# A fixed order for the first phase of a packed-attention and mixer kernel

## The chip, the cores and the metric

The kernel runs on one core of one Trainium2 chip. The metric is the device time of one execution in microseconds. A core has TensorE (matrix products and transposes, called PE in the profile), VectorE (DVE), ScalarE (ACT), GpSimd (POOL) and SyncE (SP), which only issues transfers; each runs its own instructions in its own order, and they wait for each other by semaphores. Transfers run on 16 DMA engines.

## The reference

Inputs: `q`, `k`, `v` of 8 batches x 8 heads x 576 rows x 64, and `p` of 32 rows for each head; matrices `U` (576 x 32), `V` (32 x 576), `w_ch1` (512 x 2048) and `w_ch2` (2048 x 512), these four in float64. For every batch:

```python
p_packed = sm_attn(p, k, v)            # softmax(scale * p k^T) v, 32 rows per head
out = sm_attn(q, p_packed, p_packed)   # 576 rows per head
x = out.transpose(0, 2, 1, 3).reshape(B, S, H * D)
u = x + (x^T U V)^T                    # mixing over the 576 tokens
y = u + relu(u @ w_ch1) @ w_ch2        # the output, float32
```

## The kernel before

**The first phase** computes `p_packed`. Its unit is half a batch: four heads, so there are 16 units (`UN`), two for each batch. A unit goes through these stages:

- `a_load`, `a_load_v`: K is loaded in one transfer (line 190, tile `kx`), V in five (lines 391 and 392, tile `vt`); with the first unit of a batch also the rows of `p`, in two (line 381, `pn`). K and V have three buffers each.
- `a_turn`: K is transposed on TensorE in three groups (lines 201 and 208, into `k_ps`) and copied out to `kT` by ScalarE (lines 205 and 209); with the first unit of a batch also `p` (`a_p`).
- `a_scores` (line 219): 16 small products into `s_ps`. `a_softmax` (lines 421 to 425): maxima on VectorE, exponentials on ScalarE.
- `a_turn_back` (lines 226 and 228): the exponentials are transposed back into `m_ps` and copied to `eT`.
- `a_pack` (line 451): 40 small products with V; ScalarE scales them to `two` (line 453).
- `a_heads` (line 461): one transpose, copied out by ScalarE (line 462). After the second unit of a batch other than the first, the packed rows are stored in DRAM (line 467, `ppTd`), from where `load_ppT` fetches them later.

Beside the units the phase loads `w_ch1` in 16 chunks of 512 KB (`load_w1`, line 136, issued from ScalarE) and makes float32 of them (`convert_w1`, through `float32_of`: the Abs of line 76 on ScalarE, then lines 77 to 80 on VectorE). Four chunks are in flight: two tiles `bits` and two `bits2`. It prepares `U` and `V`, does the second attention and the token mixing of batch 0 (`attention(0)`, 24 steps, called `first`), and the first piece of the folded weight (`fold(0, 0)`: the packed rows times `w_ch1`). In this phase the program's text gives no order: a planner with a cost model reorders each engine's instructions, SyncE's too, within what the data and the free buffers allow.

**The second phase** is in the order of the source (`tc.manual_schedule()`), on every engine. It loops over 8 batches and, in each, over 16 blocks `kt` of the hidden dimension. `gemm1(kt)` makes 128 hidden values of all rows from the batch's attention weights and the folded weight, split into high and low parts, so each product is three (lines 85 to 87); `gemm2(kt - 1)` multiplies by `w_ch2`. Among these products stand the steps of the next batch's attention (`steps`), the folds, in batch 0 the conversion of `w_ch2`, and the stores. Where a batch is odd, the last 64 rows of two batches are done together (`joint`).

The main lines of the first phase's loop, in the order of the source that the planner starts from:

```python
for i in range(NU + 3):
    a_turn_back(i - 1); a_scores(i)
    a_load_v(i + 1); a_turn(i + 1); a_load(i + 2)
    some_w1()                     # once or twice: convert a chunk, load another
    a_softmax(i)
    # two steps of the first attention from i = 5
    a_pack(i - 2); a_heads(i - 3)
```

Of the kernel before, what the change touches and what calls it, by code (L numbers as in the profile page):

```python
# [19 lines left out]
def packed_attention_mixer_kernel(  # L20
# [112 lines left out]
    def load_w1(n):  # L133
        x, c = chunks[n]
        b = bits["w1", n] = bits_tile() if n % 2 else sA.tile([P, 512, 2], I32, name="bits2")
        nc.scalar.dma_start(out=b.rearrange("p x t -> p (x t)"), in_=w1[P * x:P * x + P, 2 * QW * c:2 * QW * c + 2 * QW])

    def convert_w1(n):
        x, c = chunks[n]
        float32_of(conv_tile(I32), conv_tile(F32), bits.pop(("w1", n)), w1t[x][:, QW * c:QW * c + QW])  # L140
# [53 lines left out]
    def turn(t, x, h, bank):  # L194

        x = x.rearrange("p (h y) -> p h y", h=2)
        t_ps = bank()
        if h < 2:
            for j in range(4):
                o = P * (2 * (j % 2) + j // 2)  # L200
                nc.tensor.transpose(t_ps[:, o:o + P], x[:, h, P * j:P * j + P], ident)  # L201
            src = t_ps.rearrange("p (k a z i) -> p a z k i", k=2, a=2, z=2)
            for a in range(2):
                dst = t[:, 2 * h:2 * h + 2, :4 * I].rearrange("p z (k i a) -> p a z k i", k=2, a=2)[:, a]
                nc.scalar.copy(dst, src[:, a])  # L205
        else:
            for h in range(2):
                nc.tensor.transpose(t_ps[:64, P * h:P * h + P], x[:, h, SM:], ident)
            nc.scalar.copy(t[:64, :, LAST], t_ps[:64, :2 * P].rearrange("p (h i) -> p h i", h=4))
# [154 lines left out]
    actx = ExitStack()  # L364
    sA = actx.enter_context(tc.tile_pool(name="sA", bufs=2, reuse_waits="tile"))
# [19 lines left out]
    def a_load_v(u):  # L385
        b, g = UN[u]
        vt = ua[u]["v"] = sA.tile([P, 5, 4 * D], F32, name="vt", bufs=3)
        rows = v[b, 4 * g:4 * g + 4].rearrange("h (i c) d -> i c h d", c=NT)
        main = v[b, 4 * g:4 * g + 4].rearrange("h (i c) d -> h i (c d)", c=NT)[:, :, :8 * D]
        for h in range(4):  # L390
            nc.sync.dma_start(out=vt[:, h], in_=main[h].rearrange("i (a x) -> i a x", a=2))
        nc.sync.dma_start(out=vt[:64, 4].rearrange("p (h d) -> p h d", h=4), in_=rows[:, 8])
# [23 lines left out]
    def a_softmax(u):  # L416
        ss = ua[u]["s"]
        mx = sA.tile([P, 3], F32, name="mx")
        sm = ua[u]["sum"] = sA.tile([P, 2], F32, name="sm", bufs=3)
# [3 lines left out]
        e1 = ua[u]["e"] = sA.tile([P, S], F32, name="e1")  # L423
# [3 lines left out]
    def a_turn_back(u):  # L427
        e1, sm = ua[u]["e"], ua[u]["sum"]
        eT = ua[u]["eT"] = sA.tile([P, 5, P], F32, name="eT")
        t_ps = bank_a("m")()  # L430
# [3 lines left out]
        t_ps = bank_a("m")()  # L434
        turn_back(t_ps, e1, 4, 0)
        nc.vector.tensor_copy(eT[:64, 4], t_ps[:64, :P])
        rs = ua[u]["rs"] = sA.tile([P, 1], F32, name="rs")
# [3 lines left out]
    def a_pack(u):  # L441
        b, g = UN[u]
        eT, vt = ua[u]["eT"], ua[u]["v"]
        p_ps = bank_a("m")()
# [7 lines left out]
        two = ua[u]["two"] = sA.tile([P, 2, D], F32, name="two")  # L452
# [3 lines left out]
    def a_heads(u):  # L456
        b, g = UN[u]
        if g == 0:
            pps[b] = ppT_tile() if b == 0 else sA.tile([P, 2, P], F32, name="ppTa", bufs=1)
# [14 lines left out]
    a_turn(0)  # L474
    n_w1 = 0
    first = attention(0, res)

    def some_w1():
        nonlocal n_w1
        if n_w1 < 16:  # L480
            convert_w1(n_w1)
            if n_w1 + 4 < 16:
                load_w1(n_w1 + 4)
            n_w1 += 1

    for i in range(NU + 3):
        if 0 <= i - 1 < NU:
            a_turn_back(i - 1)
        if i < NU:
            a_scores(i)  # L490
        if i + 1 < NU:
            a_load_v(i + 1)
            a_turn(i + 1)
        if i + 2 < NU:
            a_load(i + 2)
        for _ in range(2 if 2 < i < 8 else 1):
# [15 lines left out]
        if i == 13:  # L512
            load_w2(0)
            load_w2(1)
        if i == 14:
            fold(0, 0)
        if i == 16:
            steps = attention(1, res)
            steps.pop(0)()
            split_w2(*convert_w2(0))  # L520
            load_w2(2)
    actx.close()


    ctx.enter_context(tc.manual_schedule())
# [3 lines left out]
    w2_tiles(sB, 2)  # L529

# [117 lines left out]
    for b in range(B):  # L648
# [3 lines left out]
        for kt in range(NK):  # L652
# [3 lines left out]
            if steps and kt % 4 != 2:  # L656
                steps.pop(0)()
            if kt > 0:
# [64 lines left out]
```

## Time and profile before

| | us |
|---|---|
| median of 3 runs | 877.29 (874.79 to 880.39) |
| profiled execution | 878.53 |
| its span, first to last instruction | 876.8 |
| TensorE busy in matrix products | 834.3 (95%) |
| VectorE, ScalarE, GpSimd busy | 380.6, 338.1, 93.4 |
| first product of `gemm1` | 131.2 |
| mean granted TensorE clock | 0.974 |

On the profile's page each engine has a row of 40 digits, one for each fortieth of the span: the digit is the busy share in tenths. PEclk is the TensorE clock that was granted, and the row DMA the mean busy share of the 16 DMA engines. A row of a group of instructions names the line, the engine, the operation, the tile written and the tiles read, the shape and the count; behind the bar stand the busy time, the mean of one in nanoseconds, and the idle time just before them with what ended it. SPq rows are SyncE issuing a transfer; the time of the transfer itself is not in them, and is given as the time from issue to landing.

### The profile page before, as it was taken

The numbers are of one execution on the slowest core, as the hardware profiler recorded it, in microseconds if no ns is written. First come the engines' busy times: TensorE is split into PE (matmuls) and PEld (weight loads), VectorE is DVE, ScalarE is ACT, GpSimd is POOL, SyncE is SP. The second block draws the span as 40 slices with busy tenths as digits, with TensorE's granted clock in tenths as the row PEclk, the third lists the DMA queues.
The fourth block names the chain that finished last, engine by engine and source line by source line (L and its number), as shares of the span: only waits on it lengthen the run. The fifth ranks groups of instructions, "written<-read, shape, count | busy, mean of one in ns | idle before, by whom it ended". The sixth has DMA issues, their size and how long they took to land.

```text
span 876.8 us, 14674 instructions
## 1 busy us (share of the span) xinstructions
PE 834.3 (95%) x5808; PEld 664.7 (76%) x5808; DVE 380.6 (43%) x924; ACT 338.1 (39%) x1064; POOL 93.4 (11%) x111
## 2 busy tenths in 40 slices
PE   4689889999999999999999999999999999999997
PEld 2445547777888888788888878788888888888886
DVE  4458647877434333433343423434243234342222
ACT  4658755434423334234323332334233332342221
POOL 0002123332011100101010101110111001010000
PEclk9779979999999999999999999999999999999999
DMA  9998842223100110011001100011001100010001
GB/s 302 275 333 277 251 139 81 80 92 109 49 1 1 61 49 13 1 35 63 12 1 60 50 13 1 1 61 49 1 1 61 49 13 1 1 49 1 1 1 61
DMA packets 38980, 59.09 MB, mean 67 GB/s; under 512 B 11776, under 2 KB 21888, under 8 KB 38912
## 3 DMA queue, kind: packets, MB, share of 16 engines
q1 hardware_dynamic: 36608, 49.77, 17.9%
q10 hardware_dynamic: 2304, 8.39, 2.7%
q8 instruction: 46, 0.75, 0.4%
q14 instruction: 22, 0.18, 0.1%
HBM read 47.79 MB, written 10.35 MB: 66 GB/s over the span
## 4 chain that ended last, share of the span: by engine, by line
PE 86%; DVE 5%; ACT 3%; DMA 3%; issue 1%; SPq 1%; POOL 0%; ACTq 0%; DVEq 0%
PE o L85 16%; PE o L86 15%; PE o L87 15%; PE h_ps L85 8%; PE h_ps L87 7%; PE h_ps L86 7%; PE t_ps L351 4%; PE t_ps L201 2%; PE t_ps L219 2%; PE m_ps L451 1%; PE k_ps L201 1%; PE t_ps L294 1%; PE s_ps L219 1%; DVE os L77 1%; DMA kx<-in_k_dram 1%
## 5 line engine op out<-in xcount | busy, mean ns | idle before, releaser
L85 PE MATMUL o<-w2h,hh 128*128 128x512 f32 x512 | 207.1, 404 | 0.0
L86 PE MATMUL o<-w2l,hh 128*128 128x512 f32 x512 | 202.1, 395 | 0.0
L87 PE MATMUL o<-w2h,hl 128*128 128x512 f32 x512 | 201.8, 394 | 0.0
L582 DVE SCALAR_TENSOR_TENSOR hl<-h_ps,hh 128x256 fp32r<-128x256 f32 x256 | 104.3, 422 | 202.5 <-ACT hj L581 189.6
L579 ACT ACTIVATE hh<-h_ps 128x256 fp32r<-128x256 f32 x256 | 99.0, 388 | 187.3 <-PE h_ps L87 186.7
L85 PE MATMUL h_ps<-ah,wth 128*128 128x320 f32 (+1 forms) x512 | 158.4, 309 | 1.9 <-DVE hl L582 1.9
L86 PE MATMUL h_ps<-al,wth 128*128 128x320 f32 (+1 forms) x512 | 152.1, 297 | 0.0
L87 PE MATMUL h_ps<-ah,wtl 128*128 128x320 f32 (+1 forms) x512 | 151.8, 297 | 0.0
L85 PEld LDWEIGHTS h_ps<-ah,wth 128*128 128x128 f32 x512 | 97.3, 190 | 33.7 <-issue 25.7
L87 PEld LDWEIGHTS o<-w2h,hl 128*128 128x128 f32 x512 | 96.8, 189 | 22.2
L85 PEld LDWEIGHTS o<-w2h,hh 128*128 128x128 f32 x512 | 97.1, 190 | 21.3 <-issue 3.6
L86 PEld LDWEIGHTS o<-w2l,hh 128*128 128x128 f32 x512 | 97.3, 190 | 16.4
L86 PEld LDWEIGHTS h_ps<-al,wth 128*128 128x128 f32 x512 | 97.4, 190 | 1.8
L87 PEld LDWEIGHTS h_ps<-ah,wtl 128*128 128x128 f32 x512 | 97.5, 190 | 0.0
L358 DVE TENSOR_TENSOR wtl<-t_ps,wth 128x256 fp32r<-128x256 f32 x128 | 48.6, 420 | 91.8 <-ACT wth L357 88.5
L357 ACT CAST wth<-t_ps 128x256 fp32r<-128x256 f32 x128 | 43.4, 375 | 111.2 <-PE t_ps L351 97.1
L314 POOL TENSOR_TENSOR al<-aT,ah 128x320 fp32r<-128x320 f32 (+1 forms) x32 | 25.6, 802 | 211.6 <-ACT ah L313 211.5
L258 POOL TENSOR_TENSOR e<-e,m 128x576 f32<-128x576 f32 x16 | 18.7, 1171 | 238.7 <-DVE m L257 238.7
L351 PE MATMUL t_ps<-w1t,ppT 64*32 64x512 f32 x512 | 37.0, 610 | 0.0
L205 ACT COPY xT<-t_ps 128x256 f32<-128x256 f32 x64 | 21.6, 398 | 36.5 <-PE t_ps L201 35.8
L313 ACT CAST ah<-aT 128x320 fp32r<-128x320 f32 (+1 forms) x32 | 13.9, 433 | 53.9 <-DVE aT L312 53.9
L77 DVE TENSOR_SCALAR os<-os 128x512 f32<-128x512 f32 (+2 forms) x35 | 22.0, 629 | 22.3 <-ACT os L76 22.3
(118 smaller groups left out, 1003.1 us busy)
## 6 DMA issues: line engine op xcount, KB each, us to landing
kx<-in_k_dram SPq DMA_DIRECT2D x16, 576.0 KB, 5.3
x<-in_q_dram SPq DMA_DIRECT2D x16, 576.0 KB, 4.8
bits<-in_moe_w_ch_dram ACTq DMA_DIRECT2D x16, 512.0 KB, 6.3
vt<-in_v_dram SPq DMA_DIRECT2D x64, 128.0 KB, 4.4
bits<-in_moe_w_ch_dram SPq DMA_DIRECT2D x16, 512.0 KB, 3.5
out_dram<-bits SPq DMA_DIRECT2D x32, 256.0 KB, 2.4
pn<-in_p_dram SPq DMA_DIRECT2D x16, 64.0 KB, 4.7
vt<-in_v_dram SPq DMA_DIRECT2D x16, 64.0 KB, 4.3
```

The source lines that it names most:

```text
L77: nc.vector.tensor_single_scalar(t, t, LEAST, op=ALU.max)
L85: nc.tensor.matmul(ps, lhsT=lh, rhs=rh, start=start, stop=False)
L86: nc.tensor.matmul(ps, lhsT=lh, rhs=rl, start=False, stop=False)
L87: nc.tensor.matmul(ps, lhsT=ll, rhs=rh, start=False, stop=stop)
L201: nc.tensor.transpose(t_ps[:, o:o + P], x[:, h, P * j:P * j + P], ident)
L219: nc.tensor.matmul(ss[r][hs, :n], lhsT=lT[rs, g, hs], rhs=t[rs, h, :n], start=True, stop=True)
L314: nc.gpsimd.tensor_tensor(al[:, g, ns], aT[:, ns], ah[:, g, ns].bitcast(F32), op=ALU.subtract)
L351: nc.tensor.matmul(f_ps[g][xs], lhsT=ppT[b][zs, g, xs], rhs=w1t[h // 2][zs, QW * c:QW * c + QW], start=True, stop=True)
L357: nc.scalar.copy(hi[:, g], f_ps[g][:, cs])
L358: nc.vector.tensor_tensor(lo[:, g], f_ps[g][:, cs], hi[:, g].bitcast(F32), op=ALU.subtract)
L579: nc.scalar.activation(hh[:, ms], src, AF.Relu)
L582: nc.vector.scalar_tensor_tensor(hl[:, ms], src, 0.0, hh[:, ms].bitcast(F32), op0=ALU.max, op1=ALU.subtract)
```

## The change

The region in the order of the source now begins ahead of the first phase, so that each engine, SyncE among them, issues its instructions as the text has them. For this the loop is rewritten: the stages of three units follow each other in a fixed order, and the loads stand behind the pack and the heads. One chunk of `w_ch1` is converted in each iteration (two in iterations 1, 5 and 9), its loads move from ScalarE's queue to SyncE's, and its Abs is issued one chunk ahead (`test_w1`). The steps of the first attention come three in an iteration, from iteration 4. The loop ends after 16 iterations in place of 19: the stages that are left of the last units (`rest`) are done among the products of the first four blocks of batch 0, in ordinary banks (`bank`). The tiles that they need are in a pool of their own (`sT`), and the last four tiles of `w_ch2` get their place after it is closed, at block 5. In batch 0 a step of the next attention may stand in every block. Of the two copies behind a group of transposes (of K, and of Q in both phases) the second goes to VectorE.

```diff
-    def float32_of(x, t, raw, out=None):
+    def float32_of(x, t, raw, out=None, tested=False):
...
-        nc.scalar.activation(t, high.bitcast(F32), AF.Abs)
+        if not tested:
+            nc.scalar.activation(t, high.bitcast(F32), AF.Abs)
...
-        nc.scalar.dma_start(out=b.rearrange("p x t -> p (x t)"), in_=w1[P * x:P * x + P, 2 * QW * c:2 * QW * c + 2 * QW])
+        nc.sync.dma_start(out=b.rearrange("p x t -> p (x t)"), in_=w1[P * x:P * x + P, 2 * QW * c:2 * QW * c + 2 * QW])
+
+    tests = {}
+
+    def test_w1(n):
+        tests[n] = conv_tile(F32)
+        nc.scalar.activation(tests[n], bits["w1", n][:, :, 1].bitcast(F32), AF.Abs)
...
-                nc.scalar.copy(dst, src[:, a])
+                if a:
+                    nc.vector.tensor_copy(dst, src[:, a])
+                else:
+                    nc.scalar.copy(dst, src[:, a])
...
     actx = ExitStack()
+    ctx.enter_context(tc.manual_schedule())
+    tctx = ExitStack()
+    sT = tctx.enter_context(tc.tile_pool(name="sT", bufs=2, side="right", reuse_waits="tile"))
...
     a_turn(0)
+    first = attention(0, res)
+    test_w1(0)
+
+    def some_w1(n):
+        convert_w1(n)
+        if n + 1 < 16:
+            test_w1(n + 1)
+        if n + 4 < 16:
+            load_w1(n + 4)
...
-    for i in range(NU + 3):
-        if 0 <= i - 1 < NU:
-            a_turn_back(i - 1)
-        if i < NU:
-            a_scores(i)
+    for i in range(NU):
+        a_scores(i)
+        a_softmax(i)
+        if i > 0:
+            a_turn_back(i - 1, bank_a("m"))
+        if i >= 4 and first:
+            first.pop(0)()
+        if i + 1 < NU:
+            a_turn(i + 1)
+        if i >= 4 and first:
+            first.pop(0)()
+        if i > 1:
+            a_pack(i - 2, bank_a("m"))
+        if i > 2:
+            a_heads(i - 3)
         if i + 1 < NU:
             a_load_v(i + 1)
-            a_turn(i + 1)
         if i + 2 < NU:
             a_load(i + 2)
-        for _ in range(2 if 2 < i < 8 else 1):
-            some_w1()
-        if i < NU:
-            a_softmax(i)
-        if i >= 5:
-            for _ in range(2):
-                if first:
-                    first.pop(0)()
-        if 0 <= i - 2 < NU:
-            a_pack(i - 2)
-        if 0 <= i - 3 < NU:
-            a_heads(i - 3)
+        for _ in range(2 if i in (1, 5, 9) else 1):
+            if n_w1 < 16:
+                some_w1(n_w1)
+                n_w1 += 1
+        if i >= 4 and first:
+            first.pop(0)()
...
+    rest = [
+        lambda: (a_pack(NU - 2, bank), a_heads(NU - 3)),
+        lambda: a_turn_back(NU - 1, bank),
+        lambda: (a_pack(NU - 1, bank), a_heads(NU - 2)),
+        lambda: (a_heads(NU - 1), tctx.close()),
+    ]
     actx.close()
...
-            if steps and kt % 4 != 2:
+            if rest:
+                rest.pop(0)()
+            elif steps and (b == 0 or kt % 4 != 2):
                 steps.pop(0)()
+            if (b, kt) == (0, 5):
+                w2_tiles(ctx.enter_context(tc.tile_pool(name="sC", bufs=1, side="right", reuse_waits="tile")), 2)
```

More of the change, by code (lines that the diff above doesn't have):

```diff
@@ L418, in a_softmax @@
         mx = sA.tile([P, 3], F32, name="mx")
-        sm = ua[u]["sum"] = sA.tile([P, 2], F32, name="sm", bufs=3)
+        sm = ua[u]["sum"] = sT.tile([P, 2], F32, name="sm", bufs=3)
         for r in range(2):
@@ L458, in a_heads @@
         if g == 0:
-            pps[b] = ppT_tile() if b == 0 else sA.tile([P, 2, P], F32, name="ppTa", bufs=1)
+            pps[b] = ppT_tile() if b == 0 else sT.tile([P, 2, P], F32, name="ppTa", bufs=1)
         z_ps = bank()
```

39 lines of the change are left out of this document (15 added, 24 removed).

## The prediction

> **What bounds the kernel now.** I read the page first, for where TensorE is not full.
>
> ```profile
> span 876.8 us, 14674 instructions
> ...
> PE   4689889999999999999999999999999999999997
> ...
> PEclk9779979999999999999999999999999999999999
> DMA  9998842223100110011001100011001100010001
> ```
>
> A slice is 21.9 us. TensorE is full from the seventh slice on; the first six (131 us) have gaps, a lower granted clock, and DMA engines that are full for three slices and then fall off. The table by windows gives this in numbers. Its columns are the window, its length, busy time of TensorE, weight load, VectorE, ScalarE and GpSimd, then clock, DMA share and GB/s.
>
> ```profile
> 20.00:30.00 10.00, 4.53 (x32) 2.80 (x33) 4.13 (x14) 3.33 (x13) 0.00 (x0) 0.61 0.99 325
> 0.00:100.00 100.00, 73.85 (x934) 43.34 (x935) 63.08 (x174) 63.33 (x206) 10.19 (x22) 0.88 0.92 293
> 131.20:224.10 92.90, 87.00 (x540) 71.48 (x541) 70.96 (x135) 44.11 (x124) 31.44 (x34) 0.96 0.27 86
> 224.10:310.50 86.40, 86.12 (x551) 70.83 (x550) 33.74 (x83) 30.96 (x99) 7.85 (x8) 1.00 0.08 28
> ```
>
> Over the first 100 us the transfers run at 293 GB/s with a share of 0.92: here loads bound the kernel. The products of batch 1 (the last row) leave TensorE 0.3 us idle; those of batch 0 leave 5.9 us. The products begin where the first product of `gemm1` stands, at 131.2:
>
> ```profile
> L85 PE MATMUL h_ps<-ah,wth x92: 280/302/468, 131.2 to 258.7; 128*128 128x320 f32 x46, 128*128 128x256 f32 x46
> ```
>
> After that the kernel needs 876.8 - 131.2 = 745.6 us, nearly all of it TensorE. The change decides when the products start; so the first phase is what has to be costed. How it keeps the DMA engines full is seen on the tile of the K loads:
>
> ```profile
> L208 PE MATMUL k_ps<-ident,kx x32: 272/298/423, 13.6 to 106.7; 128*64 128x128 f32 x32
> L190 SPq DMA_DIRECT2D kx<-in_k_dram x16: 368/419/666, 1.7 to 93.3; - x16
> DMA to landing us min/median/max: 4.2/5.3/10.1
> ```
>
> The last K load is issued at 93.3 and its last transposes start near 106.7: 13 us ahead of use, about two units. The order found by the planner moved K loads that far ahead of V loads and of the packs.
>
> **The change, part by part. The load order** carries the sum. In the new source order, iteration i runs on TensorE: scores(i), back-transposes(i-1), transposes of K(i+1), pack(i-2), heads(i-3). Only behind these does SyncE get V(i+1), then K(i+2), then a W1 chunk. V has three buffers, so V(i+1) takes that of V(i-2) and must wait for pack(i-2). K(i+2) is behind V on the same queue, and is wanted in the very next iteration by transposes that stand ahead of pack(i-1) on TensorE. That closes a ring: pack(i-2), V issues, K issue, K landing, K transposes, pack(i-1). K is one iteration ahead, not two, and the third K buffer is not used for more. SyncE's rows price its issues; its waits show that it holds what is behind a waiting issue.
>
> ```profile
> 34.30 1.22 SPq L381 DMA_DIRECT2D pn<-in_p_dram  x2
> 35.62 0.41 SPq L190 DMA_DIRECT2D kx<-in_k_dram  x1
> ...
> 42.20 2.50 SPq L391 DMA_DIRECT2D vt<-in_v_dram  x4
> 44.75 0.62 SPq L392 DMA_DIRECT2D vt<-in_v_dram  x1
> 45.47 0.55 SPq L190 DMA_DIRECT2D kx<-in_k_dram  x1
> ...
> 68.27 0.55 SPq L467 DMA_DIRECT2D ppTd<-ppTa  x1
> ```
>
> ```profile
> SPq L467 <- ACT ah L313: 8.9, 1, 8.9
> ...
> SPq L392 <- DMA kx<-in_k_dram: 4.8, 2, 2.8
> ```
>
> From the first V issue to the K issue is 45.47 - 42.20 = 3.27 us. Where a new batch starts, two P loads come between: 35.62 - 34.30 = 1.32 us. The last row, V waiting for a K landing with its own buffer still unused, is a limit on loads in flight; it matters at the start only, since a ring of over 10 us lets all of them land. TensorE's parts come from the groups of the window 0 to 131.2 (busy us, mean ns of one):
>
> ```profile
> L201 PE MATMUL k_ps<-ident,kx 128*128 128x128 f32 x128 | 23.2, 333 | 4.0 <-DMA kx<-in_k_dram 3.3 <-ACT kT L205 0.7
> L219 PE MATMUL s_ps<-kT,pT 64*32 64x256 f32 (+1 forms) x256 | 21.7, 465 | 0.0
> L451 PE MATMUL m_ps<-vt,eT 128*32 128x64 f32 (+1 forms) x640 | 18.9, 249 | 0.8 <-DVE eT L436 0.8
> L226 PE MATMUL m_ps<-ident,e 128*128 128x128 f32 x64 | 15.2, 331 | 13.4 <-ACT e L425 12.5 <-DMA pn<-in_p_dram 0.6
> L208 PE MATMUL k_ps<-ident,kx 128*64 128x128 f32 x32 | 7.2, 310 | 1.9 <-ACT kT L205 1.8
> L453 ACT ACTIVATE two<-m_ps,rs 128x128 f32<-128x128 f32 x16 | 6.0, 378 | 1.5 <-PE m_ps L451 1.3
> L461 PE MATMUL t_ps<-ident,two 128*128 128x128 f32 x16 | 5.4, 337 | 1.0 <-ACT two L453 0.5 <-DVE aT L312 0.3
> L228 PE MATMUL m_ps<-ident,e 128*64 128x128 f32 x16 | 4.9, 304 | 0.0
> L294 PE MATMUL t_ps<-x,ua 128*128 128x256 f32 (+1 forms) x10 | 3.2, 464 | 0.0
> L462 ACT COPY ppTa<-t_ps 128x128 f32<-128x128 f32 x12 | 3.0, 285 | 0.4 <-PE t_ps L461 0.4
> L201 PE MATMUL t_ps<-ident,x 128*128 128x128 f32 x16 | 3.0, 319 | 0.7 <-ACT xT L205 0.7
> ```
>
> Per unit: K transposes (23.2 + 7.2) / 16 = 1.9 us, scores 1.36, pack 18.9 / 16 = 1.18, back-transposes (15.2 + 4.9) / 16 = 1.26, heads 0.34. One turn of the ring is 3.27 + 5.3 (median landing) + 1.9 + 1.18 = 11.65 us. Scores, back-transposes and heads (3 us) lie inside the 8.6 us for which TensorE waits for K. Before, a unit took 6.2 us: the last transposes of a unit's K go from 13.6 to 106.7 in the row above, over 15 units.
>
> The ring first binds behind pack(0), in iteration 2, and last ends in pack(12), in iteration 14: 12 turns, 139.8 us. To it come:
> - P loads ahead of K in the six turns whose K begins a batch: 6 x 1.32 = 7.9.
> - From the third such turn on, the packed rows of the batch before are stored ahead of V on SyncE, and the store waits for ScalarE's `two` (0.378) and the copy behind the transpose (0.34 + 0.285), then issues in 0.55: about 1.2 us, four times, 4.8 (1.55 at most, 0.55 at least).
> - Steps of the first attention that stand between K transposes and pack: two groups of four transposes (3.0 / 4 = 0.75 each), one of scores, one of back-transposes (about 1.3 each), the mix (3.2), two small products: 7 us in all. The other sixteen steps fall in TensorE's wait for K and cost nothing unless that wait goes.
>
> Together 159.5 us. The start, until pack(0) ends: K(3) has 4 K, 3 V, 5 W1 chunks and 4 P loads ahead of or with it.
>
> ```profile
> kx<-in_k_dram SPq DMA_DIRECT2D x16, 576.0 KB, 5.3
> ...
> bits<-in_moe_w_ch_dram ACTq DMA_DIRECT2D x16, 512.0 KB, 6.3
> vt<-in_v_dram SPq DMA_DIRECT2D x64, 128.0 KB, 4.4
> ...
> pn<-in_p_dram SPq DMA_DIRECT2D x16, 64.0 KB, 4.7
> vt<-in_v_dram SPq DMA_DIRECT2D x16, 64.0 KB, 4.3
> ```
>
> That is 6,848 KB or 7.0 MB, 24 us at 293 GB/s from about 2 us on; then 1.9 and 1.18: 29 us. From pack(12) to the products: heads, scores(15), back-transposes(14), pack(13), heads: 0.34 + 1.36 + 1.26 + 1.18 + 0.34 = 4.5. The products start at 29 + 159.5 + 4.5 = 193, instead of 131.2: 62 us later.
>
> **The moved tail.** Two packs, one set of back-transposes and three heads now run among the products: 2.4 + 1.3 + 1.0 = 4.7 us of TensorE that nothing hides, since TensorE bounds there; they are 4.7 us less before. The 4.5 us above already leave them out, so they are added: +4.7 (3 at a full clock). Each stands one product block away from the next, which covers its copies.
>
> **W1 on SyncE, its Abs ahead.** The issue follows K, off the ring; it waits for VectorE to convert an older chunk, and what is queued behind it is V, which waits for a later pack anyway: 0. ScalarE drops 16 issues, and is not bound: 0.
>
> **Half the copies to VectorE.** Nearest rows for one copy, ScalarE now and VectorE from PSUM at that size:
>
> ```profile
> L205 ACT COPY kT<-k_ps 128x256 f32<-128x256 f32 x64 | 20.6, 404 | 10.3 <-PE k_ps L201 6.0 <-DMA kx<-in_k_dram 4.1
> ...
> L358 DVE TENSOR_TENSOR wtl<-t_ps,wth 128x256 fp32r<-128x256 f32 x4 | 1.7, 420 | 1.0 <-ACT wth L357 1.0
> ```
>
> In the first phase this can save 0.4 us a unit on ScalarE, behind the ring's wait. In the products VectorE gets 4 copies a batch beside 33.7 us of work in 86.4; cover is ample: 0 (bounds -1 and, wholly exposed, 28 x 0.42 = +12). **Batch 0's steps** are spread more evenly and the last weight tiles placed later: at most the 5.9 us of idleness back; I take 0.
>
> **Sum.** On the profiled execution's 878.5 us (876.8 span and 1.7 around it): 878.5 + 62 + 4.7 = 945; that execution stands 1.2 above the median, so 944.
>
> **The clock.** TensorE will sit idle for some 5 us of each turn. The row from 20 to 30 us, with TensorE busy 4.53 of 10, has a granted clock of 0.61. The Trainium skill, page "TensorE: Matmul & The Clock Gate", section "HAM oscillation", says that a loop which waits over about 3.4 us for DMA at each tile starts each tile at half clock. This row agrees; by the rule the K transposes would be cold in every turn, and the sum some 5 us more than with the mean. Another sentence speaks against the change: "DMA: Bandwidth & Descriptors" of the Trainium skill, section "Rules for kernel authors", asks to issue a load early and wait late; the 13 us of lead above agree.
>
> **The rivals.** *Loads keep their lead (0.05).* If K issues aren't held behind V's wait for the pack, loads run on at 293 GB/s as they do now, and end near 100 us. K(15) then gives TensorE transposes, scores and the 4.5 us chain: products at about 109, 878.5 - 22 + 4.7 = 861. It decides from the point where the K issue precedes the pack by a unit or more. For it: K leads by 13 us now. Against it: SyncE's 8.9 us hold above shows a queue in order, and the source puts K last.
>
> *Short landing (0.08).* With the queue empty at each V issue, K might land in the least time seen, 4.2, or less; with 3.0 as an extrapolation, 1.5 for transposes, 0.9 for packs and no exposed step, a turn is 8.7: products at 29 + 104 + 12.7 + 4.5 = 150, time 902. Against it: V's 576 KB go just ahead, 2 us at 293 GB/s. A turn shorter still, at the 6.2 us of now, is the no-change case (0.04).
>
> *Engines in order add to the ring (0.11).* Sixteen attention steps put TensorE behind VectorE or GpSimd; if each held it a further 2 us outside the wait for K, +32: 976.
>
> **How the numbers follow.** Forecast 0.72. Its own bounds: down with landing 4.2 (-13), transposes 1.5 and packs 0.9 (-8), no exposed step (-7), a store at 0.55 (-3), batch 0's idleness back (-6): 907; up with landing 6.3, as the W1 loads had (+12), transposes at half clock (+5), a us more at eight steps (+8): 969. The range 904 to 970 holds this and a part of the neighbours, about 8 in 10. Within 1% (868.5 to 886, about what a measurement here can tell from no change) is the 6.2 us turn alone, 0.04; faster 0.05; slower 0.91.
>
> **What would show it.** Right: K issues of one unit follow the pack of four units earlier by 3 to 5 us; K transposes wait for the K landing in nearly every unit; scores of successive units 11 to 14 us apart; the DMA row of the page at 4 or 5 tenths (1,664 KB in a turn of 12 to 13 us) from the second slice to the eighth; first `gemm1` near 193. Wrong: K issued before that pack, the DMA row at 9 until it ends, the first `gemm1` before 140, or products after it that differ from 745.6 by much more than 5 us.

## The result, and the profile after

The changed kernel takes 962.13 us (median of four runs, 961.24 to 965.1), the kernel before 878.13 (874.79 to 880.39) beside it. The ratio is 1.0958, with a 95% interval of 1.0922 to 1.0993: 84 us slower. The forecast was 944, in a range of 904 to 970.

The profiled execution took 961.24 us, with a span of 959.4. The page of the kernel after, the rows of its 40 slices (a slice is 24 us now):

```profile
span 959.4 us, 14633 instructions
...
PE   5545654479979999999999999999999999999998
...
PEclk8567566769999999999999999999999999999999
DMA  8564443542222001100110011001100110001001
```

TensorE is about half full for eight slices and not full before the tenth. The DMA row, which before stood at 9 for three slices and then fell off, stands at 3 to 6 from the second slice to the eighth: about the same bytes, spread over nearly twice the time (the K loads are issued until 187.6 us, before until 93.3). The table by windows of the kernel after, with the columns of the prediction's table:

```profile
0.00:100.00 100.00, 51.24 (x499) 31.77 (x500) 47.62 (x127) 36.16 (x109) 5.67 (x14) 0.68 0.64 196
100.00:204.10 104.10, 56.74 (x678) 36.20 (x676) 46.70 (x116) 37.71 (x110) 10.08 (x15) 0.66 0.46 137
204.10:303.70 99.60, 91.72 (x628) 74.76 (x629) 74.06 (x146) 45.52 (x127) 31.46 (x34) 0.95 0.26 86
303.70:390.50 86.80, 86.53 (x551) 70.91 (x550) 35.47 (x88) 29.85 (x95) 7.87 (x8) 1.00 0.08 28
```

In the first 100 us 196 GB/s are moved, against 293 before, and 137 in the second 100: loads bound nothing by their rate now. Batch 0 of the products (third row) takes 99.6 us against 92.9, batch 1 (fourth) 86.8 against 86.4. The first products of `gemm1` by their line in the kernel after:

```profile
L86 PE MATMUL h_ps<-ah,wth x512: 280/302/614, 204.1 to 936.1; 128*128 128x256 f32 x86, 128*128 128x320 f32 x85
```

The tile of the K loads in the kernel after:

```profile
L208 PE MATMUL k_ps<-ident,kx x128: 417/421/477, 6.2 to 194.1; 128*128 128x128 f32 x128
...
DMA to landing us min/median/max: 3.9/4.5/5.5
```

The products start at 204.1, not at 131.2: +72.9 us. From there to the end of the span are 755.3 us, not 745.6: +9.7. That is the whole difference of the two profiled executions (82.7).

What TensorE waited for until 204.1 (us in total, times, longest):

```profile
PE k_ps L208 <- DMA kx<-in_k_dram: 49.3, 15, 7.4
PE t_ps L411 <- DMA pn<-in_p_dram: 34.0, 8, 6.0
PE k_ps L218 <- DVE kT L213: 6.9, 3, 2.7
PE m_ps L464 <- DVE eT L449: 3.0, 1, 3.0
```

The wait for P in the kernel before, until 131.2 (that for K, 3.3, stands in the row of its line 201 above):

```profile
PE t_ps L398 <- DMA pn<-in_p_dram: 7.0, 1, 7.0
```

What SyncE's queue waited for until 204.1 in the kernel after:

```profile
SPq L480 <- ACT ppTa L475: 42.6, 5, 10.3
SPq L404 <- PE t_ps L474: 42.4, 6, 8.1
```

TensorE waited 83.3 us for loads of K and P, where it had waited 3.3 and 7.0 us. SyncE meanwhile waited 85 us, in these two rows alone, with a store or a V load at its head, and the K load behind it. (The second row names the transpose that follows the pack; in the turn below the V issue starts at 102.96, just after the pack's end and before that transpose ends, so the pack is what it waits for.) One turn of the ring, in order of time (start, duration, engine, line; the wait in brackets):

```profile
101.77 1.13 PE L464 MATMUL m_ps<-vt,eT 128*32 128x64 f32 x28
...
102.96 2.50 SPq L404 DMA_DIRECT2D vt<-in_v_dram  x4
...
106.18 0.60 SPq L197 DMA_DIRECT2D kx<-in_k_dram  x1
...
110.82 1.97 PE L208 MATMUL k_ps<-ident,kx 128*128 128x128 f32 x8 [4.43 <-DMA kx<-in_k_dram]
...
113.44 1.35 PE L464 MATMUL m_ps<-vt,eT 128*32 128x64 f32 x36
```

The pack ends at 102.9 and sets V's buffer free; five V issues and the K issue follow; K lands 4.6 us after its issue; its transposes run, with their third group at 112.88; only then comes the next pack. That is the ring of the prediction, step by step.

### The profile page after: what moved, and what is told of

Read it like the earlier page. It is cut to its first block, busy times and chain, and to the rows that moved or that the text cites. A ratio compares the mean times of both kernels' runs of the same rounds, so it can differ in the third digit from the quotient of the medians.

```text
span 959.4 us, 14633 instructions
## 1 busy us (share of the span) xinstructions
PE 849.2 (89%) x5808; PEld 677.3 (71%) x5808; DVE 410.2 (43%) x988; ACT 325.5 (34%) x1000; POOL 94.4 (10%) x111
## 4 chain that ended last, share of the span: by engine, by line
PE 80%; DMA 7%; DVE 5%; SPq 4%; ACT 2%; issue 2%; POOL 0%; ACTq 0%; DVEq 0%; POOLq 0%
PE o L86 15%; PE o L88 15%; PE o L87 15%; PE h_ps L86 8%; PE h_ps L88 7%; PE h_ps L87 7%; DMA kx<-in_k_dram 6%; PE t_ps L361 3%; SPq L404 2%; PE m_ps L464 2%; PE k_ps L208 1%; PE t_ps L208 1%; PE t_ps L229 1%; PE t_ps L304 1%; PE t_ps L236 1%
## 5 line engine op out<-in xcount | busy, mean ns | idle before, releaser
L86 PEld LDWEIGHTS o<-w2h,hh 128*128 128x128 f32 x512 | 97.5, 190 | 22.2 <-issue 4.1
L208 PE MATMUL k_ps<-ident,kx 128*128 128x128 f32 x128 | 31.4, 426 | 49.3 <-DMA kx<-in_k_dram 49.3
L208 PEld LDWEIGHTS k_ps<-ident,kx 128*128 128x128 f32 x128 | 25.1, 223 | 55.5 <-DMA kx<-in_k_dram 52.2
L213 DVE COPY kT<-k_ps 128x256 f32<-128x256 f32 x32 | 13.3, 424 | 85.0 <-ACT kT L215 85.0
```

The source lines that it names most:

```text
L86: nc.tensor.matmul(ps, lhsT=lh, rhs=rh, start=start, stop=False)
```

## The experiments

Each kernel is the kernel after with one edit, but for the last, which starts from the kernel before. The kernel after was timed once, beside the first result, and compared with that median of 962.13; the kernel before ran in every session, with medians between 877.1 and 879.6. Its turns and the start of its products vary somewhat from execution to execution (below), so 3 or 4 us of a first phase are not read as an effect, and larger ones are uncertain by that much.

**K first.** K's load moves from the end of an iteration to its head.

```diff
     for i in range(NU):
+        if i + 2 < NU:
+            a_load(i + 2)
         a_scores(i)
...
         if i + 1 < NU:
             a_load_v(i + 1)
-        if i + 2 < NU:
-            a_load(i + 2)
```

> K(i+2) is issued at the head of iteration i, ahead of V(i+1) and so ahead of V's wait for pack(i-2); nothing else moves. Ring theory: the ring opens. A turn falls from 13.6 us to what TensorE's own work takes (6.3 us of a unit at the mixed clock of before, and 1 to 2 us of attention steps), 7 to 8 us; twelve turns give back 67 to 79 us, products start at 125 to 140, time 883 to 898, TensorE's idle time before the K transposes (49.3 us, ended by K loads) below 10. Rival, order on TensorE: the phase is long because each unit's stages stand one behind another on a cold TensorE, and the load is only what it waits for last; then the gain is at most the wait of 49 us and other waits take its place, time above 925.

Measured: 908.3 us (907.3 to 910.7), 54 less than the kernel after, ratio to before 1.033 (1.0275 to 1.0384). The products start at 154.8, 49 earlier. So the place of one load on a queue is more than half of what the change costs. But the time lies between the bands of the two theories (883 to 898, and above 925): a turn took 9.7 us at the mean in place of 13.6, not 7 to 8. The waits of TensorE until 154.8:

```profile
PE k_ps L218 <- DVE kT L213: 36.8, 12, 6.3
PE k_ps L208 <- DMA kx<-in_k_dram: 11.7, 6, 4.7
```

The wait for K fell from 49.3 to 11.7, and in its place came 36.8 us of waiting for a copy out of `k_ps`, 30 more than in the kernel after. One turn of this kernel in order of time:

```profile
65.69 1.04 PE L208 MATMUL k_ps<-ident,kx 128*128 128x128 f32 x8
...
67.66 0.69 DVE L81 SCALAR_TENSOR_TENSOR w1t<-bits,os 128x512 int32<-128x512 int32 x1
...
68.93 0.81 DVE L434 TENSOR_REDUCE mx<-s_ps 128x1 f32<-128x320 f32 x2
...
70.39 0.53 ACT L438 ACTIVATE e<-s_ps,mx 128x320 f32<-128x320 f32 x1 [4.79 <-DVE mx L435]
...
72.08 0.68 ACT L215 COPY kT<-k_ps 128x256 f32<-128x256 f32 x2
...
72.59 0.75 DVE L213 COPY kT<-k_ps 128x256 f32<-128x256 f32 x2
...
73.06 0.64 PE L218 MATMUL k_ps<-ident,kx 128*64 128x128 f32 x2 [6.34 <-DVE kT L213]
```

K is transposed by 66.7. Its copies are behind the exponentials on ScalarE; these wait for the maxima; the maxima stand behind the conversion of a W1 chunk on VectorE (line 81 is its last operation). A third queue in order took over where the first was opened.

**K ahead of V, both behind the pack.** Only the two loads change places in the text.

```diff
-        if i + 1 < NU:
-            a_load_v(i + 1)
         if i + 2 < NU:
             a_load(i + 2)
+        if i + 1 < NU:
+            a_load_v(i + 1)
```

> K(i+2) and V(i+1) change places behind the pack. Ring theory: the ring stays but is shorter by V's five issues, 3.27 us a turn; 12 turns give -39 us, time 920 to 928, products near 165. K may also land some tenths earlier, with no V ahead of it. Rival, order on TensorE: less than -15.

Measured: 918.0 us (916.8 to 918.7), 1.0435 (1.0381 to 1.0489): 44 less, where twelve times the five V issues (3.27) are 39. The numbers nearly agree, but not for the reason expected. TensorE's waits until the products start, at 164.0:

```profile
PE k_ps L218 <- DVE kT L213: 33.5, 11, 6.3
PE k_ps L208 <- DMA kx<-in_k_dram: 15.9, 8, 5.4
```

With 9.1 us for P, the loads cost TensorE 25.0 us in place of 83.3, and the copies 33.5 in place of 6.9: this is the picture of K first, not that of a shorter ring. One K issue of this kernel, with the pack and the V issues after it:

```profile
100.49 0.43 SPq L197 DMA_DIRECT2D kx<-in_k_dram  x1
...
103.63 0.95 PE L464 MATMUL m_ps<-vt,eT 128*32 128x64 f32 x40
...
104.65 3.25 SPq L404 DMA_DIRECT2D vt<-in_v_dram  x4
```

K goes out 4 us before that pack ends. Nothing ties K to the pack but its place on SyncE's queue, and there K(i+2) now stands ahead of V(i+1), as in K first; only a store of packed rows, where there is one, still stands ahead of it. So this run opens the ring a second time, with the stores left ahead of K (10 us more than K first), and does not show the price of the V issues. The 3.27 us are seen in the turn of the kernel after alone (102.9 to 106.18).

**Four V buffers.** V(i+1) no longer needs the buffer of V(i-2). To make room, K has two buffers and P one.

```diff
-            pn[b] = sA.tile([P, 2, 2, D], F32, name="pn")
+            pn[b] = sA.tile([P, 2, 2, D], F32, name="pn", bufs=1)
-        ua[u]["x"] = sA.tile([P, 2 * S], F32, name="kx", bufs=3)
+        ua[u]["x"] = sA.tile([P, 2 * S], F32, name="kx", bufs=2)
-        vt = ua[u]["v"] = sT.tile([P, 5, 4 * D], F32, name="vt", bufs=3)
+        vt = ua[u]["v"] = sT.tile([P, 5, 4 * D], F32, name="vt", bufs=4)
```

> Four V buffers (K has two and p one in exchange, which the order does not use more of), so V(i+1) waits for pack(i-3), done an iteration earlier; the order of the source is unchanged. Ring theory: the hold goes in the turns without a store; in the four iterations in which the packed rows are stored, the store still stands ahead of V and K on SyncE and waits for the copy behind pack(i-2) and heads, so these four turns keep 12 to 14 us. Eight turns at 7 to 8: 45 to 52 us less, time 905 to 925. Rival, order on TensorE: above 940.

Measured: 934.7 us (934.3 to 935.4), 1.0626 (1.0572 to 1.0681): 27.5 less, between the bands of the two theories. The products start at 178.8. The waits of TensorE until then:

```profile
PE k_ps L218 <- DVE kT L213: 30.4, 10, 6.3
PE t_ps L411 <- DMA pn<-in_p_dram: 23.3, 6, 5.6
PE k_ps L208 <- DMA kx<-in_k_dram: 16.3, 10, 3.4
```

Some turns took 7 to 9 us, others 12 to 15. Four of the long ones follow a store of packed rows, which still stands ahead of V and K on SyncE and waits for a pack; not all of them do. The W1 loads, which the change moved to SyncE, stand ahead of V and K as well, and wait for a conversion on VectorE:

```profile
SPq L137 <- DVE w1t L81: 28.1, 9, 6.5
```

In the kernel after this wait is 6.3 us, three times. So V's buffer was one link of the ring among several, and the copy wait comes out here too. One P buffer may have added to the 23.3 us; that wasn't separated.

**A warm TensorE.** 24 transposes of the identity stand ahead of K's transposes in every turn.

```diff
+        if 2 < i + 1 < NU:
+            idle = bank()
+            for n in range(24):
+                nc.tensor.transpose(idle[:, P * (n % 4):P * (n % 4) + P], ident, ident)
         if i + 1 < NU:
             a_turn(i + 1)
```

> 24 transposes of the identity without use stand ahead of the K transposes from the second unit on, 2.6 us at a full clock and 5.1 at half, about as much as TensorE's idle time there. What they add to the work is no part of the computation. Clock theory (the turn's transposes, pack and steps cost more than at a full clock because TensorE idles): K transposes 1.5 instead of 2.75, pack 0.9 instead of 1.4, per turn -1.8; 12 turns give -15 to -25 us, time 937 to 947. If the clock costs nothing: 962 or, where the added work is not hidden, up to 975.

Measured: 956.3 us (952.5 to 959.3), 1.0857 (1.0785 to 1.0928): 6 less, between what the two theories gave. The windows until 201.7, where the products start:

```profile
0.00:100.00 100.00, 66.80 (x645) 47.75 (x645) 47.76 (x128) 36.62 (x109) 5.81 (x14) 0.85 0.62 197
100.00:201.70 101.70, 72.96 (x844) 52.87 (x842) 46.96 (x116) 37.28 (x109) 9.76 (x15) 0.80 0.46 141
```

The group of K's transposes in the same time (busy us, mean ns, idle before):

```profile
L208 PE MATMUL k_ps<-ident,kx 128*128 128x128 f32 x128 | 27.1, 380 | 26.3 <-DMA kx<-in_k_dram 26.3
```

The granted clock rose from 0.68 and 0.66 to 0.85 and 0.80, a K transpose went from 426 to 380 ns, half way to the 333 of before; the twelve turns went from 163.2 to 161.2 us, and the transfers kept their rate. The low clock comes with the idle time, since work put into it raised the clock. What it costs by itself stays open: only five of the sixteen groups of K's transposes came to 1.04 to 1.26 us (the others took 1.9 or more, as all sixteen do in the kernel after), and the added transposes have a cost.

**K's transposes ahead of the scores.** K first as above, and the turn of K is issued ahead of the scores, so that its copies don't stand behind the exponentials; once with the copies as in the kernel after, once with both on ScalarE.

```diff
+        if i + 2 < NU:
+            a_load(i + 2)
+        if i + 1 < NU:
+            a_turn(i + 1)
         a_scores(i)
...
-        if i + 1 < NU:
-            a_turn(i + 1)
...
-        if i + 2 < NU:
-            a_load(i + 2)
```

> As the kernel with K ahead of V, and besides the transposes of K(i+1) with their copies stand at the head of iteration i, ahead of scores(i) and softmax(i). That kernel came to 908 with TensorE waiting 37 us for VectorE's copy behind the K transposes, ten times, up to 6.3 us. Theory: in source order this copy queues on VectorE behind softmax(i), which waits for scores(i) and stands behind the conversion of W1; ahead of them the wait is under 10 us, a turn 7 to 8 us, products at 125 to 135, time 877 to 890. Rival, VectorE's work itself is too much where W1 is converted (wherever the copy stands it comes behind 2 to 5 us of conversion): the wait stays over 25 us, time above 900.

> As the run before it, with both copies on ScalarE as before the change. Theory, order: the same within 5 us in the first phase (two ScalarE copies in a row cost 0.4 a group, VectorE's conversion is no longer in the way in iterations 1, 5 and 9), and the products 0.4 us a batch shorter if the copies on VectorE cost that: 870 to 888. Rival, VectorE's work: 15 us or more faster than the run before it.

Measured: 921.0 us (920.1 to 921.6), 1.0494 (1.0455 to 1.0532), and 913.1 (911.3 to 915.7), 1.0407 (1.0366 to 1.0448). Both missed: slower than K first alone. The waits of TensorE until 159.8, in the second:

```profile
PE k_ps L208 <- DMA kx<-in_k_dram: 14.6, 7, 5.1
PE k_ps L215 <- ACT kT L212: 10.0, 7, 4.3
```

The copy wait did shrink, from 36.8 to 23.6 in the first and 10.0 in the second, but K is now wanted earlier, and four waits of 9 to 15 us share the loss (the other two: P's landing 10.0, VectorE's copy of `eT` 9.1). Ordering one wait away made others of its size.

**Copies on ScalarE.** The one change that concerns both phases is undone.

```diff
-                if a:
-                    nc.vector.tensor_copy(dst, src[:, a])
-                else:
-                    nc.scalar.copy(dst, src[:, a])
+                nc.scalar.copy(dst, src[:, a])
```

> The changed kernel with both copies on ScalarE, nothing else. Products of batches 1 to 7 take 0.4 us more each in the changed kernel than before; if the copies on VectorE are the cause, they come back to the times of before and the kernel is 3 us faster in them. In the first phase the ring theory gives 0 to +0.4 a turn (the second of two copies in a row ahead of the third group), +5 at most: 957 to 965. If the extra 0.4 us has another cause, products as in the changed kernel: 962 to 967.

Measured: 951.6 us (950.5 to 953.4), 1.0846 (1.0813 to 1.0879): 10.5 less, better than either theory. The products start at 199.4, and batch 0 by windows:

```profile
199.40:295.90 96.50, 89.51 (x627) 73.05 (x628) 73.29 (x142) 46.41 (x131) 31.44 (x34) 0.97 0.26 89
```

Batch 0 gets back 3.1 of the 6.7 us that it had lost: the kernel after has a wait of TensorE for VectorE's copy of `xT` there, 2.0 us, that is gone, and the first 20 us of the batch run at a granted clock of 0.92 and 1.00 in place of 0.83 and 0.83. The later batches keep their 0.4 us each, so those have another cause. That the 4.7 us at the start of the products are the copies' is not shown: TensorE's waits for the copies out of `k_ps` are no shorter (7.4 us, 6.9 in the kernel after), and in the experiment on the weight tiles below, whose first phase is that of the kernel after, the products started at 200.7.

**A step of the first attention out of the ring.** The step between K's transposes and the pack goes behind the pack.

```diff
-        if i >= 4 and first:
-            first.pop(0)()
         if i > 1:
             a_pack(i - 2, bank_a("m"))
         if i > 2:
             a_heads(i - 3)
+        if i >= 4 and first:
+            first.pop(0)()
```

> The changed kernel with the second attention step of each iteration behind pack and heads, out of the ring, instead of between K transposes and pack. By the term of the sum in the prediction 7 us come off: 952 to 959. If the steps hold the ring by more than their own TensorE time (waits for VectorE and GpSimd in order): 940 to 950.

Measured: 954.5 us (953.4 to 955.7), 1.0881 (1.0834 to 1.0927): 7.7 less, where the prediction's term was 7. TensorE waited 22.2 us less for K and P, and 5.6 more for the copies of `kT`; the moved step now runs in the time of those waits.

**All named waits mended at once.** K first, the copies on ScalarE, the W1 conversion behind the softmax, the pack between the groups of K's transposes, two of the three steps of an iteration behind the heads and V's load.

```diff
+        if i + 2 < NU:
+            a_load(i + 2)
         a_scores(i)
         a_softmax(i)
+        for _ in range(2 if i in (1, 5, 9) else 1):
+            if n_w1 < 16:
+                some_w1(n_w1)
+                n_w1 += 1
...
-            a_turn(i + 1)
+            a_turn_part(i + 1, (0, 1))
...
+        if i + 1 < NU:
+            a_turn_part(i + 1, (2,))
```

> Source order, with the waits that the runs so far named taken out together: K(i+2) issued at the head of iteration i; both copies on ScalarE; W1's conversion directly behind softmax(i), so that the maxima of the next softmax don't queue behind it; pack between the second and third group of K transposes; the attention steps behind pack and heads. If these waits were what kept K-first at 908: a turn is TensorE's own 6.3 us and 1 to 1.5 of steps, products at 122 to 130, then about 750: 870 to 885, even with the kernel before. If a fixed order with in-order engines costs more than the named waits (each wait removed gives room to another, TensorE stays at a clock of 0.7): 890 to 905.

Measured: 900.8 us (900.2 to 902.9), 1.0247 (1.0195 to 1.0298). This is in the rival's band: still 23 us behind the planner's order. The products start at 146.0; TensorE's waits until then are of another kind again:

```profile
PE m_ps L461 <- ACT eT L443: 19.1, 9, 5.8
```

No order by hand that was tried here came to the planner's; the best lost 15 us until the first product. Whether a fixed order exists that does is open.

**The last weight tiles on the other side.** The four last tiles of `w_ch2`, which the change allocates at block 5 on the right side of the memory, go to the left, as before.

```diff
-                w2_tiles(ctx.enter_context(tc.tile_pool(name="sC", bufs=1, side="right", reuse_waits="tile")), 2)
+                w2_tiles(ctx.enter_context(tc.tile_pool(name="sC", bufs=1, reuse_waits="tile")), 2)
```

> The changed kernel with the last w_ch2 tiles in the same memory side as the other tiles of the second phase, nothing else. In the changed kernel products with these tiles (blocks 8 to 15) take 395 to 405 ns where they took 390 to 400 before, those of blocks 0 to 7 are as before. If the place of the tiles causes it: blocks 8 to 15 as before, batches 1 to 7 0.4 us shorter each, 3 us in all: 959. If not: 962, and the 0.4 us stay.

Measured, in one execution: 954.66 us. One batch of the products (batch 3) by windows of this kernel:

```profile
485.80:572.20 86.40, 86.12 (x552) 70.83 (x551) 35.64 (x89) 29.85 (x95) 7.87 (x8) 1.00 0.08 28
```

Its products with the high part of `w_ch2`, as a group (busy us, mean ns):

```profile
L86 PE MATMUL o<-w2h,hh 128*128 128x512 f32 x64 | 25.9, 404 | 0.0
```

The same batch of the kernel after:

```profile
L86 PE MATMUL o<-w2h,hh 128*128 128x512 f32 x64 | 26.0, 407 | 0.0
```

Those with the low part took 393 ns here and 395 there. TensorE's 86.53 us in a batch (its row above is batch 1) are 86.12 again, the figure of before. So the place of these tiles is the cause of some 0.4 us in each of the batches 1 to 7, 3.0 in all. The other 3 to 4 us of this execution stand ahead of the products, at 200.7 against 204.1; with one execution and the same order they are not read as an effect.

**The tail in a row again.** The rest of the last units is done ahead of the products, as before, in the fixed order.

```diff
     actx.close()
+    for step in rest:
+        step()
+    rest = []
```

> The changed kernel with the left-over stages of the last units done in a row ahead of the products, as a tail of the first phase. By the prediction's term they cost TensorE 4.7 us in either place: batch 0 shorter by 4 to 7, the first phase longer by 4.7 and by the waits for copies between dependent stages, 2 to 5: 962 to 967. If the moved stages hold the products by more than their own time: 955 to 961.

Measured: 965.3 us (962.9 to 966.6), 1.0966 (1.0901 to 1.1032). The products start at 208.9. By the medians that is 3 us more than the kernel after, as expected for work that costs the same in either place. The traces give more, since they can be compared from the end of pack(12) on: to the end of the span this kernel needs 769.4 us (195.4 to 964.8), the kernel after 762.7 (196.7 to 959.4). The tail takes 6.1 us more ahead of the products (13.5 in place of 7.4), and behind their start nothing is won back (755.9 against 755.3): the first four blocks now carry steps of the next attention, and TensorE has a gap of 4.2 us at their transposes that it didn't have. So in the fixed order too the moved tail, with the steps that give way to it, is worth 3 to 7 us.

**The tail alone, in the planner's order.** From the kernel before: the planner orders the first phase, W1 stays on ScalarE's queue and the copies on ScalarE; the loop ends after 16 iterations, the rest stands among the products, batch 0's steps are spread as in the change, and the last weight tiles come at block 5 on their usual side. What stood in iterations 13 to 16, and the first of the attention steps, comes one to three iterations earlier.

```diff
-    for i in range(NU + 3):
+    for i in range(NU):
...
+    rest = [
+        lambda: (a_pack(NU - 2, bank), a_heads(NU - 3)),
+        lambda: a_turn_back(NU - 1, bank),
+        lambda: (a_pack(NU - 1, bank), a_heads(NU - 2)),
+        lambda: (a_heads(NU - 1), tctx.close()),
+    ]
...
-            if steps and kt % 4 != 2:
+            if rest:
+                rest.pop(0)()
+            elif steps and (b == 0 or kt % 4 != 2):
```

> One part of the change alone: the first phase keeps the planner's order, W1's loads stay on ScalarE's queue and both copies on ScalarE, as before; only the left-over stages of the last units are done among the products of batch 0, the attention steps of batch 0 are spread as in the change and the last w_ch2 tiles placed at block 5 (on the side where their products cost what they cost before). In the kernel before, 15 us pass from the last unit's scores (116) to the products (131), of which 4.7 are TensorE time of these stages and the rest waits between dependent stages and the first fold and mixing. Theory: what a tail in a row waits for is hidden among products: products start at 120 to 126, batch 0 takes 4 to 6 more than 92.9: 870 to 877, faster than both. Rival, the tail is worth nothing (in the fixed order it was shown as even within 3 us) or the planner, with one phase fewer to fill its gaps, leaves new ones: 877 to 884.

Measured: 866.95 us (865.2 to 868.2), beside 877.1 for the kernel before: ratio 0.9882 (0.9839 to 0.9925). This beats both kernels. The first products of `gemm1` and the last transposes of K (least, median and most ns, first and last start), each by its own view:

```profile
L86 PE MATMUL h_ps<-ah,wth x512: 280/302/468, 114.5 to 840.5; 128*128 128x256 f32 x86, 128*128 128x320 f32 x85
```

```profile
L215 PE MATMUL k_ps<-ident,kx x32: 272/273/423, 13.8 to 106.8; 128*64 128x128 f32 x32
```

And the windows of the first 100 us and of batch 0:

```profile
0.00:100.00 100.00, 74.94 (x1005) 45.51 (x1005) 66.95 (x183) 66.95 (x217) 9.95 (x22) 0.98 0.93 295
114.50:211.00 96.50, 89.99 (x629) 73.52 (x628) 70.90 (x140) 46.09 (x131) 30.22 (x28) 0.96 0.28 92
```

The transfers run at 295 GB/s as before, and the last transposes of K begin at 106.8, as before (106.7). Before, 24.5 us lay between these and the first product of `gemm1`; now 7.7 do. The products start 16.7 us earlier and batch 0 takes 96.5 us against 92.9: 13 us are won in the profiled executions and 10 in the medians. So one part of the change is a gain where the loads keep their lead, more than the theory expected (870 to 877). The spread of batch 0's steps was not tried without it.

## Why the prediction was right, and where it was short

**The ring** stands as forecast. K's issue of a unit follows the pack four units earlier by 3.3 us in the turn shown (3 to 5 forecast). TensorE waited 15 times for K and 8 times for P. The packs of successive units end 11.9 to 15.2 us apart, five of the twelve over 14; 11 to 14 were forecast for the scores. The DMA row was forecast at 4 or 5 tenths from the second slice to the eighth and is between 3 and 6. From the end of pack(0), at 33.5, to that of pack(12), at 196.7, are 163.2 us where 159.5 were worked out. Taking K from behind V's wait moved the products 49 us ahead (K first) and 40 (K ahead of V), and taking away V's wait itself moved them 25 (four V buffers). None of them came back to the 6.2 us a unit of before, so the ring is not the whole of what the order costs. The rule that the prediction set against the change (the Trainium skill, page "DMA: Bandwidth & Descriptors", section "Rules for kernel authors": issue early, wait late) agrees with these runs: 54 us for one load issued earlier.

That sum was near because its terms erred both ways. The landing of K is 4.5 us at the median, not 5.3: twelve turns are 9.6 shorter. K's transposes and a pack are longer, as their groups until 204.1 show:

```profile
L208 PE MATMUL k_ps<-ident,kx 128*128 128x128 f32 x128 | 31.4, 426 | 49.3 <-DMA kx<-in_k_dram 49.3
...
L464 PE MATMUL m_ps<-vt,eT 128*32 128x64 f32 (+1 forms) x560 | 18.4, 292 | 3.0 <-DVE eT L449 3.0
...
L213 DVE COPY kT<-k_ps 128x256 f32<-128x256 f32 x32 | 13.3, 424 | 85.0 <-ACT kT L215 85.0
...
L218 PE MATMUL k_ps<-ident,kx 128*64 128x128 f32 x32 | 9.9, 413 | 8.5 <-DVE kT L213 6.9
```

The transposes are (31.4 + 9.9) / 16 = 2.6 us a unit, not 1.9, 8 us more over twelve turns; a pack is 18.4 / 14 = 1.3, not 1.18, 1.6 more. The durations had been taken at the clock of the kernel before. "Transposes at half clock" stood in the prediction as an upper bound of 5 and should have been the term: the ring itself makes the idle time. The Trainium skill, page "TensorE: Matmul & The Clock Gate", section "HAM oscillation", says that a loop with waits over about 3.4 us starts each tile at half clock; the median transpose of K, 421 ns against 272 at the least before, agrees with it, and so do its sixteen groups of eight, which took 1.94 to 1.97 us each (1.04 the fastest in the run with a warm TensorE). In the run with a warm TensorE the transposes of the two rows of K took 4.7 us less in all, and the twelve turns 2.0 less. The step term agrees with its run: 7 us for the steps in the ring, and 7.7 measured when one of the three an iteration was taken out of it, give or take the 3 or 4 us of the first phase. The term of 3.27 for the V issues was confirmed in the turn alone, not by a run. With the three corrections (the landing, the transposes, the pack) the sum is 159.5 again: that it came so near is in part luck, and the 3.7 us by which the turns were longer were not separated.

**Where 16 us were missing.** On the profiled executions 945 was forecast and 961.2 came. Five places make this up: the start until pack(0) 4.5 (33.5, not 29), the turns 3.7, the chain from pack(12) to the products 2.9 (7.4, not 4.5), batch 0 2.0 (6.7, not 4.7), and the later batches 3.0 (not foreseen). Batch 0's 6.7 and the later batches' 3.0 are the 9.7 us by which the time behind the start of the products differs from 745.6; the prediction had named much more than 5 there as a sign of being wrong.

- *The start* was worked out as 7.0 MB at 293 GB/s. Until pack(0) ends, TensorE also waits 5.3 us for VectorE's copies of `kT`, twice (part of the 6.9 in the row above), which had no term; how much of the 4.5 they make was not separated.
- *The chain to the products* was a sum of TensorE's work. It leaves out the wait of pack(13) for VectorE's copy of `eT`: 3.0 us, once, the fourth row of the waits above. That is about the whole of the 2.9.
- *Batch 0.* Its moved work measures 3.9 us (two packs 1.9, the back-transposes 0.9, three heads 1.1), nearer to the 3 at a full clock than to the 4.7 taken. With the copies on ScalarE the batch is 3.6 longer than before. So the tail was priced 1.1 too high, and the copies' 3.1 were missing.
- *Half of the copies to VectorE* was costed at 0, with bounds of -1 and +12. Undoing it gave 10.5 us back in the medians, 3.1 of them in batch 0; how much of the rest is the spread of the first phase is open. The step that failed is "cover is ample": VectorE's free time did not keep TensorE from waiting 2.0 us for a copy of `xT` among the products.
- *Later weight tiles* were taken as at most a gain, "idleness back". That their place in memory changes the products' time was not thought of: 3.0 us.

**W1 on SyncE at 0** was not tried by itself and stays open. While the ring binds, the runs agree with it: SyncE waited 6.3 us with a W1 load at its head, ahead of a V load that had a later pack to wait for. With V's wait gone (four V buffers) the same loads held the queue for 28.1 us. VectorE's conversion in W1's way did prove costly, but for the exponentials behind it, and only once the ring was open.

**The rivals.** "Loads keep their lead" and "no change" are refuted: K's issue stands behind the pack. "Short landing" had the direction of the landing right (4.5, with 3.9 the least) but not its size. "Engines in order add to the ring" was given 976 as an addition; the runs show something else: waits behind VectorE and ScalarE, for copies rather than for attention steps, were small while the ring bound (6.9 and 3.0 us in the rows above), and came out in its place when it was opened. Of the 72.9 us by which the products start later, K first gave back 49, and 30 us more of waiting for copies came up.

## What to carry to other kernels

A load that stands behind a load which waits for a buffer has that buffer's release in its path: before an order is fixed, follow each queue, SyncE's above all, and look whether the wait closes a ring with the engine that must release it. When such a ring is opened, expect the next queue in order to take over, and price it before the gain is counted. Separate the parts of a large change: here a kernel that was 84 us slower held a part that by itself made it 10 us faster. And compare the waits as well as the times: K ahead of V came within 2 us of what was expected of it, by another way than the one expected.

## What the runs showed of the hardware

- Two engines that copy the two halves of one bank run one after the other. In the group row of line 213 above, all 85.0 us of VectorE's idle time ahead of its copy are ended by ScalarE's copy; a pair took 0.39 and then 0.42 us (from 99.98 and from 100.40), with none of it together. It is not the common destination: VectorE's copy from one bank, until 100.82, and ScalarE's from the next, from 100.78, overlap. The Trainium skill, page "PSUM — Partial Sum Buffer", section "PSUM bank collisions raise a hardware error", says that the compiler keeps ScalarE and VectorE apart where they touch one bank in the same quarter of the partitions; this trace agrees.
- The place of a weight tile in the memory changed the 128x512 products that read it, 404 and 393 ns to 407 and 395 on the mean of a batch, with nothing else edited. Why is open.
- Work added into TensorE's idle time raised its granted clock in the first phase from 0.68 and 0.66 to 0.85 and 0.80, and the kernel with it was 6 us faster in spite of that work.
